# First five pairs' scores in unsplit float32, weight words on GpSimd, early scores in either half of PSUM, and eight spare matmuls of the identity

## The chip, the cores and the metric

The kernel runs on one core of a Trainium2 chip. The metric is device time in microseconds, the median of several runs. A core has five engines with a queue each, worked through in order: PE (TensorE, matrix products into PSUM), DVE (VectorE), ACT (ScalarE), POOL (GpSimd, which doesn't reach PSUM) and SP, which here issues the DMAs. Waits are on semaphores, so an instruction that waits holds up all that stand behind it on its engine.

## The reference

For 8 batches, attention over 8 heads of 576 positions and 64 dimensions, with a threshold close under the row maximum; its output, 576 x 512 per batch, is then mixed over tokens and channels with sines and cosines.

```python
scores = scale * np.matmul(q, k.transpose(0, 1, 3, 2))
thresh = np.max(scores, axis=-1, keepdims=True) - tau
scores = np.where(scores >= thresh, scores, -1000000000.0)
attn = np.exp(scores - np.max(scores, axis=-1, keepdims=True))
attn = attn / (np.sum(attn, axis=-1, keepdims=True) + 1e-09)
x = heads_side_by_side(np.matmul(attn, v))
theta = x @ w_theta
y = w_tok_r @ (x * np.cos(theta)) + w_tok_i @ (x * np.sin(theta))
u = x + y
return u + np.maximum(u @ w_ch, 0.0)
```

The last three steps are taken for each batch. The three weights `w_theta`, `w_tok_r`/`w_tok_i` (both in `w_tok`) and `w_ch` come as float64, 8 bytes a number; all else is float32.

## The kernel before

Two heads make a pair, so there are 32 pairs, 4 to a batch, numbered n = 0 to 31. All numbers are float32, but PE multiplies most of them as "float32r", a rounded form that goes through in one pass. Where accuracy is needed a number x is split into a rounded part and the rest, x = x1 + x2, and the product is taken as x1 y1 + x1 y2 + x2 y1: three one-pass products in place of one plain float32 product.

- `prepare_q` and `prepare_k` load a pair's q and k into `rawq` and `rawk`, round them (a cast on DVE, L705 and L722, or on ACT, L707 and L724) and take the rest (a subtraction, L530, on DVE or POOL). From pair 3 on, DVE first multiplies q by a scalar (`gate`, L696); for pairs 0 to 2 that scalar is applied with the scores.
- `unit(n, i)` takes 128 query rows of both heads (i = 0 to 3) or the last 64 of both (i = 4). PE writes the scores (L759): 12 matmuls of 64 rows x 288 columns, the two heads' each in one half of the array's rows, into four PSUM banks, always banks 0 to 3. DVE copies each head's scores out of PSUM and takes the row extremum along (L780), adds the threshold (L790); ACT makes two passes over them (L804, L811); DVE transposes the result in blocks of 32 (L823, L825) into `a`. "A head" below is one such 128 x 576 block; a pair has 9.
- `values(n)` multiplies `a` by v (L840, 72 plain float32 matmuls on 32-row tiles a call), also into banks 0 to 3. `divide(n)` spreads the inverse row sums over DRAM and multiplies them in (L894, L900).
- `convert` makes two float32r parts of a float64 weight chunk, 13 chunks early on: 4 of `w_theta`, 9 of `w_tok` (4 of `w_ch` follow later). ACT takes the magnitude of the high words (L578), POOL clamps it (L583), DVE builds the float32 bits (L597, L604), the scale of the low word (L611) and the low word times that scale (`word`, L615). ACT rounds the bits (L626); PE adds up bits + word - rounded (L634 to L636), and ACT copies the rest out (L640).
- `mixture(b)` follows once the 4 pairs of a batch are done: channel products (`product`, L948), sines on ACT, transposes (L1091) and the token products (L1136), again with split operands. The first L948 is the first work on PE that needs weights.

Nothing is scheduled at run time: every instruction group is an `Op` in a list, and `ORDER` gives the sequence in which they are emitted, as steps forth and back in that list. `PLACES` gives, for each kind of buffer (`bank` is the PSUM banks), which one each use takes. So the order on every engine is a table of numbers.

## Time and profile before

| | |
|---|---|
| median of 3 runs | 926.42 us (924.15 to 927.21) |
| profiled execution, its own time | 924.78 us |
| its span, first to last instruction | 923.0 us |
| PE, DVE, ACT, POOL busy | 866.0, 714.4, 699.5, 314.3 us |
| mean granted TensorE clock | 0.989 of full speed |

Busy time of PE is modelled for pipelined matmuls, so that it is not PE at its peak. Idle time of an engine that isn't the bottleneck costs nothing. A wait is put down to the releaser that came last.

### The profile page before, as it was taken

The numbers are of one execution on the slowest core, as the hardware profiler recorded it, in microseconds if no ns is written. First come the engines' busy times: TensorE is split into PE (matmuls) and PEld (weight loads), VectorE is DVE, ScalarE is ACT, GpSimd is POOL, SyncE is SP. The second block draws the span as 40 slices with busy tenths as digits, with TensorE's granted clock in tenths as the row PEclk, the third lists the DMA queues.
The fourth block names the chain that finished last, engine by engine and source line by source line (L and its number), as shares of the span: only waits on it lengthen the run. The fifth ranks groups of instructions, "written<-read, shape, count | busy, mean of one in ns | idle before, by whom it ended". The sixth has DMA issues, their size and how long they took to land.

```text
span 923.0 us, 34024 instructions
## 1 busy us (share of the span) xinstructions
PE 866.0 (94%) x14632; PEld 779.5 (84%) x14632; DVE 714.4 (77%) x1598; ACT 699.5 (76%) x1406; POOL 314.3 (34%) x390
## 2 busy tenths in 40 slices
PE   4778799999999999999999999998999999999998
PEld 3556688788898988988999989897989989989898
DVE  7998889987787887778877887777975886876443
ACT  5788898865897678965899659976797659975540
POOL 0212451613443244513244343342334442321202
PEclk9988999999999999999999999999999999999999
DMA  7356535355342364024534351434534243423502
GB/s 261 115 161 224 166 138 178 101 167 178 131 158 93 131 209 175 17 80 151 201 103 144 110 187 67 170 107 143 183 129 129 82 146 122 138 83 131 164 22 75
DMA packets 62375, 126.15 MB, mean 137 GB/s; under 512 B 22512, under 2 KB 31632, under 8 KB 58128
## 3 DMA queue, kind: packets, MB, share of 16 engines
q1 hardware_dynamic: 62080, 123.97, 40.2%
q8 instruction: 115, 1.88, 0.8%
q14 instruction: 36, 0.29, 0.1%
q10 hardware_dynamic: 144, 0.00, 0.0%
HBM read 110.17 MB, written 13.78 MB: 134 GB/s over the span
## 4 chain that ended last, share of the span: by engine, by line
PE 64%; DVE 20%; ACT 8%; issue 3%; DMA 3%; POOL 1%; SPq 0%; DVEq 0%; POOLq 0%; ACTq 0%
PE banks_ps__66 L1136 21%; PE banks_ps__66 L840 14%; PE banks_ps__66 L948 13%; PE banks_ps__66 L759 11%; DVE sc L780 7%; DVE a L823 5%; PE banks_ps__66 L1091 3%; ACT sc L804 2%; ACT s L811 2%; DVE nm L790 1%; PE banks_ps__66 L634 1%; DMA z<-in_w_theta_dram 1%; DVE xl L530 1%; DVE z L1016 1%; DVE zl L1116 1%
## 5 line engine op out<-in xcount | busy, mean ns | idle before, releaser
L804 ACT ACTIVATE sc<-sc,nm 128x576 f32<-128x576 f32 x288 | 216.7, 771 | 78.6 <-DVE nm L790 75.1
L811 ACT ACTIVATE s<-sc,small 128x576 f32<-128x576 f32 x288 | 222.9, 775 | 5.1 <-DVE a L823 0.6
L823 DVE STREAM_TRANSPOSE a<-s 128x576 f32<-128x576 f32 x256 | 189.7, 759 | 35.3 <-PE banks_ps__66 L840 28.6
L759 PE MATMUL banks_ps__66<-k,q 64*128 64x288 f32 (+1 forms) x1728 | 178.7, 320 | 32.7 <-DVE sc L780 24.0
L780 DVE TENSOR_SCALAR_CACHE_REDUCE sc<-banks_ps__66 128x576 f32<-128x576 f32 x261 | 186.2, 741 | 13.2 <-PE banks_ps__66 L759 11.5
L759 PEld LDWEIGHTS banks_ps__66<-k,q 64*128 64x128 f32 (+1 forms) x1728 | 141.4, 194 | 61.1 <-DVE sc L780 37.9
L948 PE MATMUL banks_ps__66<-xh,wm 128*128 128x288 f32 x1024 | 168.9, 302 | 4.2 <-issue 1.6
L840 PE MATMUL banks_ps__66<-a,v 32*64 32x144 f32 x9216 | 165.0, 288 | 4.9 <-DVE sc L780 3.9
L1136 PE MATMUL banks_ps__66<-wt_h,zh 128*128 128x288 f32 x576 | 164.4, 309 | 1.7 <-DVE xT L1148 1.2
L840 PEld LDWEIGHTS banks_ps__66<-a,v 32*64 32x64 f32 x9216 | 146.9, 132 | 18.0 <-issue 9.2
L1136 PE MATMUL banks_ps__66<-wt_l,zh 128*128 128x288 f32 x576 | 160.6, 302 | 0.0
L948 PEld LDWEIGHTS banks_ps__66<-xh,wm 128*128 128x128 f32 x1024 | 143.4, 188 | 14.6 <-issue 8.6
L1066 POOL TENSOR_TENSOR z<-z,xT 128x288 f32<-128x288 f32 x112 | 91.7, 850 | 118.9 <-ACT z L1047 96.4
L1136 PEld LDWEIGHTS banks_ps__66<-wt_h,zh 128*128 128x128 f32 x576 | 108.9, 190 | 6.9 <-issue 3.9
L1136 PEld LDWEIGHTS banks_ps__66<-wt_l,zh 128*128 128x128 f32 x576 | 108.6, 189 | 2.8 <-issue 2.6
L530 POOL TENSOR_TENSOR k<-rawk,k 128x288 fp32r<-128x288 f32 x62 | 52.9, 860 | 168.5 <-DVE k L722 93.0
L530 POOL TENSOR_TENSOR xl<-xT,xh 128x288 fp32r<-128x288 f32 x78 | 66.8, 878 | 109.6 <-ACT xh L907 67.6
L1136 PE MATMUL banks_ps__66<-wt_h,zl 128*128 128x288 f32 x576 | 95.8, 301 | 0.0
L948 PE MATMUL banks_ps__66<-xl,wm 128*128 128x288 f32 x512 | 92.6, 300 | 2.9 <-issue 2.7
L1116 DVE TENSOR_TENSOR zl<-banks_ps__66,zh 128x512 fp32r<-128x512 f32 (+1 forms) x96 | 51.9, 547 | 56.1 <-ACT zh L1097 56.0
L1136 PEld LDWEIGHTS banks_ps__66<-wt_h,zl 128*128 128x128 f32 x576 | 81.5, 188 | 2.9 <-issue 2.4
L948 PEld LDWEIGHTS banks_ps__66<-xl,wm 128*128 128x128 f32 x512 | 75.0, 188 | 7.1 <-issue 6.0
(78 smaller groups left out, 996.3 us busy)
## 6 DMA issues: line engine op xcount, KB each, us to landing
v<-in_vp_dram SPq DMA_DIRECT2D x32, 1152.0 KB
wm<-wm_dram SPq DMA_DIRECT2D x64, 512.0 KB
rawq<-in_qT_dram SPq DMA_DIRECT2D x31, 320.0 KB
rawk<-in_kT_dram SPq DMA_DIRECT2D x31, 288.0 KB
out_dram<-xT SPq DMA_DIRECT2D x31, 288.0 KB
rb<-sums_dram SPq DMA_DIRECT2D x64, 128.0 KB
z<-in_w_tok_dram SPq DMA_DIRECT2D x9, 576.0 KB
wm_dram<-rb SPq DMA_DIRECT2D x16, 256.0 KB
```

The costliest lines, as they stand in the source:

```text
L530: eng.tensor_tensor(out=out()[:, c0:c1], in0=in0()[:, c0:c1], in1=in1()[:, c0:c1], op=ALU.subtract)
L759: nc.tensor.matmul(ps()[:, 2 * j + h, :HS], q[a]()[r, i * P : (i + 1) * P], k[c]()[r, h * HS : (h + 1) * HS], start=(x == 0), stop=(x == 2),)
L780: lambda j=j, sc=sc, scaled=scaled: nc.vector.tensor_scalar(out=sc().rearrange("p (a b) -> p a b", a=2), in0=ps()[:, 2 * j : 2 * j + 2, :H ...
L804: lambda j=j, sc=sc: nc.scalar.activation(out=sc(), in_=sc(), func=AF.Prelu, bias=nm()[:, 2 + j : 3 + j], scale=-1.0, alpha=STEEP),
L811: lambda j=j, sc=sc, total=total, weights=weights: nc.scalar.activation(out=weights(), in_=keys(sc()), func=AF.Exp, bias=back, accum_out=p ...
L823: nc.vector.transpose(out=a()[:, :, j, 32 * i : 32 * i + 32], in_=src.rearrange("p (c q) -> p c q", q=32))
L840: nc.tensor.matmul(ps()[64 * h : 64 * h + 64, b, :w], v()[r, c, h, :], a()[r, c, h, :], start=(c == 0), stop=(c == 17))
L948: nc.tensor.matmul(ps[h]()[:, :HS], wm()[:, a, c, :], parts[c][bb]()[:, h * HS : (h + 1) * HS], start=first and n == 0, stop=final and n = ...
L1066: eng.tensor_tensor(out=zi, in0=zi, in1=x[m]()[:, c0:c1], op=ALU.mult)
L1091: nc.tensor.transpose(out=tp()[:, i * P : (i + 1) * P], in_=z()[:, c : c + P], identity=ident)
L1116: lambda zh=zh, zl=zl, tv=tv: nc.vector.tensor_tensor(out=zl(), in0=tv(), in1=zh().bitcast(F32), op=ALU.subtract),
L1136: nc.tensor.matmul(ps()[:, :HS], zz[c][lo]()[:, zz[c][2]], w[:, c, hs], start=(q + n == 0), stop=(q + n == len(work) - 1),)
```

## The change

For pairs 0 to 4 (`WHOLE = 5`) q and k aren't split: they are loaded straight into the buffers from which PE reads, and the scores are plain float32 products, 4 matmuls to a full unit in place of 12. Pairs 1 to 4 get `gate` multiplied in on POOL, so that only pair 0 applies it with the scores. For the same pairs (`TWICE = 5`) scores and values may stand in banks 0 to 3 or 4 to 7. In `convert`, the first 10 of the 13 early chunks have the low word's product on POOL, as a cast and a product for each half of the chunk, and the first 8 also the rounding of the bits; the factor 2^-52 goes into the matrix that PE multiplies by. `awake` is a matmul of the identity by itself, 256 columns, whose result nobody reads; there are eight of them. `PLACES` and `ORDER` are new all the way through.

```diff
     "wm": (
-        "0101201220220101200012012001201201201201022100121010210210012012011200"
+        "0101201010110202100121021000211021201210210221010210210210201212011201"
...
-    one = const.tile([P, P], F32R, name="one")
-    nc.scalar.copy(out=one, in_=ident)
+    unit_low = const.tile([P, P], F32R, name="unit_low")
+    nc.scalar.mul(out=unit_low, in_=ident, mul=2.0**-52)
...
-        if turn < AT["wp"]:
-            for i in range(2):
-                gps(c_pool(n // 2), lambda i=i: word(nc.gpsimd, n * i // 2, n * (i + 1) // 2), key, (raw, mag), ((w, i),))
-        else:
-            dve(c_two(n), lambda: word(nc.vector), key, (raw, mag), (w,), lock=True)
+        if turn < WORD_POOL:
+            for i in range(2):
+                r = slice(n * i // 2, n * (i + 1) // 2)
+                gps(
+                    c_pool(n // 2) * 0.6, lambda r=r: nc.gpsimd.tensor_copy(out=w()[:, r], in_=lb()[:, r]), key, (raw,),
+                    ((w, i),),
+                )
+                gps(
+                    c_pool(n // 2),
+                    lambda r=r: nc.gpsimd.tensor_tensor(
+                        out=w()[:, r], in0=w()[:, r].bitcast(F32), in1=mb()[:, r].bitcast(F32), op=ALU.mult
+                    ),
+                    key, ((w, i), mag), ((w, i),),
+                )
...
-        act(c_act(n), lambda: nc.scalar.copy(out=hi(), in_=bb().bitcast(F32)), key, (bits,), (hi_b,), hold)
+        if turn < HI_POOL:
+            gps(c_pool(n) * 0.5, lambda: nc.gpsimd.tensor_copy(out=hi(), in_=bb().bitcast(F32)), key, (bits,), (hi_b,), hold=hold)
+        else:
+            act(c_act(n), lambda: nc.scalar.copy(out=hi(), in_=bb().bitcast(F32)), key, (bits,), (hi_b,), hold)
...
-                nc.tensor.matmul(t, one, w()[:, r], start=False, stop=False)
+                nc.tensor.matmul(t, unit_low, w()[:, r], start=False, stop=False)
...
+        if n < WHOLE:
+            q = sb("q", [P, QS])
+            pr.q = (q, q)
...
+            if n:
+                gps(
+                    c_pool(QS) * 0.5, lambda: nc.gpsimd.tensor_scalar(out=q(), in0=q(), scalar1=gate, scalar2=None, op0=ALU.mult), key,
+                    ((q, 0), small_b), ((q, 0),),
+                )
+            return
...
+            places=((0, 4) if n < TWICE else (0,)) if i < 4 else (0, 2), wide=2 * len(heads),
...
-        terms = ((0, 0), (0, 1), (1, 0))
+        whole = n < WHOLE
+        terms = ((0, 0),) if whole else ((0, 0), (0, 1), (1, 0))
...
+    def awake():
+        ps = bank()
+        pe(
+            0.45,
+            lambda: nc.tensor.matmul(
+                ps()[:, :256].rearrange("p (a b) -> p a b", a=2), ident, ident.unsqueeze(1).broadcast_to([P, 2, P]), start=True, stop=True
+            ),
+            0.0, (), (ps,), 4,
+        )
...
+    for _ in range(8):
+        awake()
```

Lines below L450 are numbered higher in the changed kernel: L759 is L801 there, L840 is L882, L780 is L822, L790 is L832, L823 is L865, L583 is L587, L597, L604 and L611 are L601, L608 and L615; L622, L627 and L641 are the new casts, products and roundings on POOL, L714 the product of q and `gate`, L1292 `awake`.

The first place is PE from the program's start. In the kernel before it opens with the scores of the first pair and of 2 units of the second:

```order
L759 MATMUL banks_ps__66<-k,q 128x288 x78
L840 MATMUL banks_ps__66<-a,v 64x144 x72
L871 MATMUL banks_ps__66<-ident,rows 9x128
L634 MATMUL banks_ps__66<-xh,ident 128x512
L635 MATMUL banks_ps__66<-xh,one 128x512
```

In the changed kernel PE begins so:

```order
L1292 MATMUL banks_ps__66<-ident 128x256 x3
L801 MATMUL banks_ps__66<-k,q 128x288 x18
L651 MATMUL banks_ps__66<-xh,ident 128x512
L652 MATMUL banks_ps__66<-xh,unit_low 128x512
L653 MATMUL banks_ps__66<-rb,minus 128x512
L801 MATMUL banks_ps__66<-k,q 128x288 x8
L1292 MATMUL banks_ps__66<-ident 128x256
L882 MATMUL banks_ps__66<-a,v 64x144 x72
```

Three matmuls of the identity now stand first, a pair's scores are 18 matmuls in place of 54, and the first weight chunk is summed up after the first pair's scores, ahead of the first values. Up to the first L948, PE has 252 matmuls L759 before (4 pairs and 3 units) and 90 now (5 pairs); 576 of L840 and 22 weight sums stand ahead of it in both.

The second place is DVE, where the scores begin. Before:

```order
L722 CAST k<-rawk 128x288
L530 TENSOR_TENSOR k<-rawk,k 128x288
L722 CAST k<-rawk 128x288
L705 CAST q<-rawq 128x128
L530 TENSOR_TENSOR q<-rawq,q 128x128
L530 TENSOR_TENSOR k<-rawk,k 128x288
L705 CAST q<-rawq 128x512
L530 TENSOR_TENSOR q<-rawq,q 128x512
L780 TENSOR_SCALAR sc,nm<-banks_ps__66,small 128x576 x2
L705 CAST q<-rawq 128x640
```

Now:

```order
L822 TENSOR_SCALAR sc,nm<-banks_ps__66,small 128x576 x2
L832 TENSOR_SCALAR nm<-nm,small 128x2
L822 TENSOR_SCALAR sc,nm<-banks_ps__66,small 128x576 x2
L832 TENSOR_SCALAR nm<-nm,small 128x2
L601 TENSOR_SCALAR xh<-xl 128x512
L608 SCALAR_TENSOR_TENSOR xh<-wm,xh 128x512
L865 STREAM_TRANSPOSE a<-s_119 128x18x32
L822 TENSOR_SCALAR sc,nm<-banks_ps__66,small 128x576
L615 TENSOR_SCALAR xl<-xh 128x512
```

The splits ahead of and between the scores are gone, and the first weight chunk is worked on after two units; before, that was after six and a half.

The third place is POOL, behind the making of the identity. Before:

```order
L530 TENSOR_TENSOR k<-rawk,k 128x288 x2
L583 TENSOR_SCALAR xl<-xl 128x256 x6
L583 TENSOR_SCALAR xl<-xl 128x288
L530 TENSOR_TENSOR k<-rawk,k 128x288 x2
L583 TENSOR_SCALAR xl<-xl 128x288
```

Now:

```order
L622 CAST xh<-wm 128x256
L587 TENSOR_SCALAR xl<-xl 128x256 x2
L641 CAST rb<-xh 128x512
L622 CAST xh<-wm 128x256
L627 TENSOR_TENSOR xh<-xh,xl 128x256 x2
L714 TENSOR_SCALAR q<-q,small 128x640
L587 TENSOR_SCALAR xl<-xl 128x256
```

The subtractions of k's rest have given way to casts, products and roundings of the weight words and the scaling of q. Over the whole program POOL gets 20 casts, 20 products, 8 roundings and 4 scalings, and loses 8 subtractions of k and 2 of q.

## Rows read from the trace of the kernel before

**Rows 1.** Windows: stretch, length; busy us (count) of each engine; PEclk, DMA share, GB/s.
```profile
0.00:114.70 114.70, 82.26 (x1497) 63.78 (x1497) 99.62 (x230) 89.25 (x184) 28.41 (x52) 0.93 0.57 184
114.70:200.00 85.30, 80.77 (x1332) 71.12 (x1335) 74.92 (x158) 75.31 (x151) 35.35 (x39) 1.00 0.46 149
...
sum 923.00, PE 866.00 PEld 779.48 DVE 714.42 ACT 699.53 POOL 314.28; mean PE 144.33 PEld 129.91 DVE 119.07 ACT 116.59 POOL 52.38
```
**Rows 2.** Waits in 0 to 114.7 us: who for whom: us, times, longest.
```profile
PE banks_ps__66 L759 <- DVE sc L780: 20.1, 16, 2.5
ACT sc L804 <- DVE nm L790: 13.9, 10, 7.0
...
DVE sc L780 <- PE banks_ps__66 L759: 6.6, 11, 1.2
```
**Rows 3.** Groups of DVE, 0 to 114.7 us: busy us, mean ns; idle before, releasers.
```profile
L823 DVE STREAM_TRANSPOSE a<-s 128x576 f32<-128x576 f32 x33 | 24.5, 762 | 2.2 <-ACT s L811 1.3 <-PE banks_ps__66 L840 0.9
L780 DVE TENSOR_SCALAR_CACHE_REDUCE sc<-banks_ps__66,small 128x576 f32<-128x576 f32 x27 | 21.0, 810 | 4.7 <-PE banks_ps__66 L759 4.5
L780 DVE TENSOR_SCALAR_CACHE_REDUCE sc<-banks_ps__66 128x576 f32<-128x576 f32 x13 | 9.3, 748 | 2.3 <-PE banks_ps__66 L759 2.0 <-ACT wt_l L640 0.2
L615 DVE SCALAR_TENSOR_TENSOR xh<-z,xl 128x576 fp32r<-128x576 uint32 (+1 forms) x11 | 8.0, 743 | 0.1
...
L597 DVE TENSOR_SCALAR xh<-xl 128x576 uint32<-128x576 uint32 (+1 forms) x13 | 6.5, 516 | 0.2 <-PE banks_ps__66 L636 0.2
...
L530 DVE TENSOR_TENSOR q<-rawq,q 128x640 fp32r<-128x640 f32 (+2 forms) x5 | 3.4, 687 | 0.1
...
L722 DVE CAST k<-rawk 128x576 fp32r<-128x576 f32 (+1 forms) x5 | 2.0, 398 | 0.6 <-DMA rawk<-in_kT_dram 0.6
L696 DVE TENSOR_SCALAR rawq<-rawq,small 128x640 f32<-128x640 f32 x3 | 1.6, 548 | 0.0
L705 DVE CAST q<-rawq 128x640 fp32r<-128x640 f32 (+2 forms) x4 | 1.6, 405 | 0.0
...
L530 DVE TENSOR_TENSOR k<-rawk,k 128x288 fp32r<-128x288 f32 x2 | 0.9, 455 | 0.0
```
**Rows 4.** Timeline of DVE at the start: start us, us, instruction.
```profile
4.56 0.30 DVE L722 CAST k<-rawk 128x288 fp32r<-128x288 f32 x1
...
7.61 0.82 DVE L780 TENSOR_SCALAR_CACHE_REDUCE sc<-banks_ps__66,small 128x576 f32<-128x576 f32 x1
...
8.36 0.81 DVE L780 TENSOR_SCALAR_CACHE_REDUCE sc<-banks_ps__66,small 128x576 f32<-128x576 f32 x1
```
**Rows 5.** Timeline of PE: two groups of scores.
```profile
5.76 1.81 PE L759 MATMUL banks_ps__66<-k,q 64*128 64x288 f32 x12 [5.76 <-DVE q L705]
...
38.99 1.07 PE L759 MATMUL banks_ps__66<-k,q 64*128 64x288 f32 x12 [1.07 <-ACT xT L856]
```
**Rows 6.** The chain that ended last, two pieces: start us, us, what.
```profile
84.40 0.48 PE banks_ps__66 L634 x2
...
85.15 2.44 PE banks_ps__66 L840 x144
```
**Rows 7.** Groups of POOL, 0 to 114.7 us, columns as in Rows 3.
```profile
L583 POOL TENSOR_SCALAR xl<-xl 128x288 f32<-128x288 f32 (+1 forms) x26 | 11.6, 463 | 44.2 <-ACT xl L578 30.3 <-DMA rb<-sums_dram 9.9 <-issue 4.0
L530 POOL TENSOR_TENSOR k<-rawk,k 128x288 fp32r<-128x288 f32 x9 | 7.7, 862 | 28.9 <-DVE k L722 12.0 <-ACT k L724 8.5 <-PE banks_ps__66 L840 8.4
```
**Rows 8.** Timeline of DVE and POOL about 54 us.
```profile
53.74 0.79 POOL L530 TENSOR_TENSOR k<-rawk,k 128x288 fp32r<-128x288 f32 x1
...
53.76 1.08 DVE L597 TENSOR_SCALAR xh<-xl 128x576 uint32<-128x576 uint32 x1
```
**Rows 9.** Groups of ACT, 0 to 114.7 us, columns as in Rows 3.
```profile
L811 ACT ACTIVATE s<-sc,small 128x576 f32<-128x576 f32 x39 | 30.0, 769 | 0.5
L804 ACT ACTIVATE sc<-sc,nm 128x576 f32<-128x576 f32 x40 | 30.0, 769 | 13.9 <-DVE nm L790 13.9
...
L626 ACT CAST wt_h<-xh 128x576 fp32r<-128x576 f32 x9 | 6.0, 664 | 2.9 <-DVE xh L604 2.9
```

More of the change, by code (lines that the diff above doesn't have):

```diff
@@ L686, in prepare_q @@
         pr = pairs[n]
+        if n < WHOLE:
+            q = sb("q", [P, QS])
+            pr.q = (q, q)
+            for i, (c0, c1) in enumerate(pieces_q(n)):
+                load(
+                    lambda r=slice(c0, c1): nc.sync.dma_start(q()[:, r], qT[n // NP, n % NP][:, r]),
+                    (key if n else -95.0 + 4 * i) + A("raw", n), (), ((q, i),), (c1 - c0) // 2,
+                )
[5 more added lines that the diff above has]
+            return
         raw = sb("rawq", [P, QS])
@@ L714, in prepare_k @@
         pr = pairs[n]
+        if n < WHOLE:
+            k = sb("k", [P, S])
+            pr.k = (k, k)
+            for i, (c0, c1) in enumerate(pieces_k(n)):
+                load(
+                    lambda r=slice(c0, c1): nc.sync.dma_start(k()[:, r], kT[n // NP, n % NP][:, r]),
+                    (key if n else -96.0 + 2 * i) + A("raw", n), (), ((k, i),), (c1 - c0) // 2,
+                )
+            return
         raw = sb("rawk", [P, S])
@@ L760, in score @@
                             ps()[:, 2 * j + h, :HS], q[a]()[r, i * P : (i + 1) * P], k[c]()[r, h * HS : (h + 1) * HS],
-                            start=(x == 0), stop=(x == 2),
+                            start=(x == 0), stop=(x == len(terms) - 1),
                         )
-        pe(
-            6 * c_mm(HS), score, t0 + A("score", n), [
-                *((q[0], c) for c, (c0, _) in enumerate(pieces_q(n)) if c0 <= i * P),
-                *((q[1], [(c, d) for d in range(AT["cut"])]) for c, (c0, _) in enumerate(pieces_q(n)) if c0 <= i * P),
-                k[0], k[1],
-            ],
-            ((ps, list(heads)),),
-            12 * len(heads), mode="r" if i < 4 else "m",
+        pieces = [c for c, (c0, _) in enumerate(pieces_q(n)) if c0 <= i * P]
+        if whole:
+            R = [*((q[0], c) for c in pieces), k[0]]
+        else:
+            R = [*((q[0], c) for c in pieces), *((q[1], [(c, d) for d in range(AT["cut"])]) for c in pieces), k[0], k[1]]
+        pe(
+            0.97 if whole else 6 * c_mm(HS), score, t0 + A("score", n), R, ((ps, list(heads)),),
+            (8 if whole else 12) * len(heads), mode="r" if i < 4 else "m",
         )
```

87 lines of the change are left out of this document (47 added, 40 removed), and 261 rows, old and new, of the table ORDER.

## The prediction

> **What bounds the kernel now.** I read the table of windows first, cut at 114.7 us, where PE starts its first L948 (the chain of waits puts a piece of L948 there). It splits the run in two. From there to the end PE is busy 866.00 - 82.26 = 783.74 of 808.3 us, so it waits for 24.6 us in all: this part is as long as PE's own work. Up to there PE is idle 32.4 us and DVE is busy 99.62 of 114.7 us, ACT 89.25, POOL only 28.41 [rows 1]. The waits of that stretch say who holds whom: PE's scores wait 20.1 us for DVE to have read the banks before, ACT waits 13.9 us for DVE's L790, DVE waits 6.6 us for PE [rows 2]. So the opening is DVE's, and the rest PE's. What DVE is spared in the opening moves the whole rest forward; what happens on DVE, ACT or POOL behind it counts only if PE runs dry. So I work out when the first L948 comes now, and add what PE has still to do then.
>
> **What leaves DVE's opening.** From the groups of DVE [rows 3]:
> - The splits of pairs 0 to 4: subtractions of q 3.4 and of k 0.9 us, all casts of q 1.6 (L705), four of the five casts of k 2.0 - 0.5 = 1.5 (the fifth is pair 5's), and two of three scalings, 2 x 0.548 = 1.1. Sum 8.5 us.
> - The word: 10 of 13 L615 at 0.743 = 7.4 us.
> - L780 with the scalar from memory takes 810 ns, without it 748; 18 of the 27 lose it: 18 x 0.062 = 1.1 us.
>
> Together 17.0 us by the rows. But one instruction's end overlaps the next one's start: two L780 that take 0.82 us stand 0.75 apart [rows 4]. So a tenth goes off: 15.3 us.
>
> At the very start the saving is smaller. Between 4.56 and 7.61 us DVE splits pair 0 [rows 4], and PE starts at 5.76 with 1.81 us of work [rows 5]. Now PE can start when the loads are in (by 4.6 us, since the first cast ran then) and needs some 2.2 us, so DVE's first L780 comes at 6.8, not 7.61: 0.8 us are won where 3.1 x 0.9 = 2.8 of the splits were counted. That takes 2.0 back: 13.3 us.
>
> **The second half of PSUM.** With the next scores already written, DVE should not wait for PE between units: the 6.6 us in 11 waits [rows 2] go, but for one, the first; 6.0 us. Between 0 (if the wait is for something else by then) and 6.6.
>
> **What comes in on DVE before the same point.** The order has 90 score matmuls at 18 a pair ahead of the first L948, 5 pairs and 45 heads; before it was 4 pairs and 3 units with 2 heads each, 42, of which DVE had done 40 (27 + 13) [rows 3]. Five heads more cost 5 x (0.748 + 0.762) x 0.9 = 6.8 us of DVE. They aren't lost: 252 matmuls of 1728 stood ahead, now 90 of 1548, so PE has 18 fewer to do behind, at 12 in 1.07 us [rows 5] 1.6 us.
>
> **What PE pays.** A float32 matmul of 288 columns is two records, 0.48 us at full clock [rows 6]. If the two heads run side by side, as the one-pass ones do, a unit is 2 x 0.48 = 0.96 us plus the same overhead; 12 one-pass matmuls took 1.07 late and 1.81 at the start [rows 5], with the same operands and shapes, so the rate there was lower, whatever the granted clock's mean of 0.93 over the stretch says [rows 1] (full is 2.4 GHz, the lower level 1.2). So 1.2 against 1.07, 2.2 against 1.81: 25 units x 0.15 to 0.4 = 4 to 10 us, and eight identity matmuls of under 0.5 each (256 columns against 288) some 4. PE has 32.4 us idle there to put them in: nothing on the path. Side by side is likely: the values' 144 records of 144 columns, also float32 on part of the rows, take 2.44 us, 17 ns each [rows 6], which is far less than one after the other could.
>
> **What POOL pays, and gives back to DVE.** Neither the casts nor the products are in the trace. The nearest rows: a one-input L583 463 ns, a two-input L530 862 ns [rows 7]. 20 casts at 0.463, 20 products at 0.862, 8 roundings of twice the width at 0.9 and 4 scalings at 1.0 are 37.7 us; 10 subtractions at 0.862 go: +29, POOL at 57 of some 105 us. The bounds for a cast are 0.4 and 0.86 (+8 us): it still fits. But DVE and POOL hinder each other: an L597 that starts 20 ns after a POOL L530 takes 1.08 us, its group's mean being 0.516, so one such meeting costs DVE 0.57 [rows 3, 8]. With POOL's load doubled I take five more of them than before: 3 us. The bounds are none, and all 39 of L597, L611 and L604: 22 us.
>
> The Trainium skill (SBUF — State Buffer, section Who interferes with whom) says that the two engines share a port pair as an exclusive lock, held for a whole instruction, so that a DVE instruction in a two-port mode or with two SBUF inputs blocks and is blocked. By that rule these 39 and nothing from PSUM are exposed; the row about 54 us agrees with it, and 3 us is the sum's value by the rows alone.
>
> ACT: 8 of 13 roundings go, 8 x 0.664 = 5.3, and five heads come, 5 x 2 x 0.769 = 7.7, both times 0.9: 89.25 - 4.8 + 6.9 = 91.4 us [rows 1, 9]. It starts after the first L790, now near 9 us, so it can't be through before 100.4. ACT's first instruction is now the magnitude of a weight chunk, ahead of the first pair's exponentials; that chunk's load stands fifth on SP, behind only pair 0's q and k, so I count no wait, with 2.5 us as the upper bound (DVE then stalls at its first L597).
>
> **Sum.** -13.3 - 6.0 + 6.8 + 3.0 = -9.5: first L948 at 105.2, above ACT's 100.4. With -1.6 behind it, -11.1. The later part has an order of its own, but the same instructions; I leave its 24.6 us of waits as they are. The profiled execution took 924.78 us, its span 923.0; so 913.7 for one like it. The median of the runs stands 1.6 above the profiled one (926.42): 915.3, and I say 915.5.
>
> **Rivals.**
> - ACT or POOL becomes the opening's bound. ACT's 100.4 leaves 4.8 us for waits, and in before it waited 6.9 us for L790 besides the first 7.0 [rows 2]; POOL's words take 2 x 0.862 where DVE's took 0.743, in a queue with the scaling of q. If ACT keeps 6.9 and 3 more for POOL's results, the first L948 is at 110.3: -4.4 - 1.6 = -6.0, 920. Against it: DVE, which made ACT wait, is lighter.
> - More comes of it: no meetings, and DVE's lighter load also takes 3 of the 4.5 us of PE's waits between 114.7 and 200 [rows 1]: -9.5 - 3.0 - 1.6 - 3 = -17, 909; ACT's floor sets the end at 100.4 - 114.7 - 1.6 - 3 = -19, 907.
> - Slower: DVE and POOL in each other's way, at L597, L611 and L604 of the 13 chunks. Each full meeting is 0.57 us; without the 3 us counted the gain is 14.1, so from 25 of 39 on nothing is left, and all 39 give 22 - 14 = +8: 934. Against it: L597's mean of 0.516 says that few of 13 met one [rows 3], at a third of POOL's load to come.
> - The float32 scores don't run side by side. Then a unit is 1.92 us at full clock, 25 units 48 us instead of some 30: PE gets near 100 us of work ahead of L948 and the gain is some 3 us, 922; with much of it at the lower rate, 3.84 a unit, PE needs 25 us more than it has: 945.
> - The order after the opening waits more: if 24.6 us grow by a third, 8 us are given back, 923.5, which reads as no change.
>
> **Chances.** Forecast 0.50, its own range 909 to 921; ACT or POOL bound 0.20; more 0.13; port meetings 0.06; no side by side 0.04; later waits 0.07. The range from 905 to 924 leaves out the two slower cases, the lower end of the third, and little else. About 0.3% (2.8 us) is what a measurement of this kernel can tell from no change. Faster by more: the first three nearly whole and a part of the last two, 0.83; within: most of the last and the edge of the second, 0.09; slower: the meetings and half of no side by side, 0.08.
>
> **What would show it.** The first L948 (now L990) near 105 us. DVE's busy share before it above 0.92, with L780 (L822) no longer waiting for PE. A score unit in float32 near 1.2 us late and 2.2 early: twice that means that the heads follow one another. L597 (L601) with a mean above 0.7 us would mean the port rival; ACT idle less than 5 us after its start, the ACT one. PE idle behind the first L948 near 24 us; above 32 us there, the last rival holds. I'm wrong if the first L948 comes after 112 us, or if it comes at 105 and the end doesn't follow.

## The result and the profile after

The changed kernel takes 914.75 us (median of 4 runs, 913.64 to 915.14) against 926.82 us (924.15 to 927.38) for the one before beside it. The ratio is 0.9873, interval [0.9852, 0.9895]. The forecast was 915.5 us. By the medians the gain is 12.1 us; the two profiled executions, from which all that follows is read, differ by 923.0 - 913.2 = 9.8, as the one before was 2.0 us quicker than its median. Lines of the changed kernel: scores L801 (before L759), their copies L822 (L780), threshold L832 (L790), values L882 (L840), transposes L865 (L823), bits L601, L608, L615 (L597, L604, L611), product of the mixture L990 (L948); on POOL the word's cast and product are L622 and L627, the rounding L641, the scaling of q L714.

The stretches ahead of and behind the first L990, after (it starts at 104.9 us, the last one at 909.0):

```profile
0.00:104.90 104.90, 83.43 (x1441) 59.19 (x1441) 94.88 (x214) 85.20 (x177) 60.21 (x95) 0.95 0.61 203
104.90:909.00 804.10, 781.82 (x13115) 714.27 (x13114) 617.35 (x1357) 606.52 (x1218) 281.23 (x338) 1.00 0.39 130
```

And the second stretch of the kernel before, first product to last:

```profile
114.60:918.80 804.20, 782.99 (x13133) 715.15 (x13132) 614.33 (x1368) 610.39 (x1223) 285.97 (x340) 1.00 0.39 130
```

The whole gain of the profiled executions lies ahead of the first product: 114.6 - 104.9 = 9.7 us. Behind it both kernels take the same 804 us, PE being busy for 782 and 783 of them. POOL's busy time in the opening has doubled, from 28.41 to 60.21 us [rows 1].

Waits in the first 104 us, after, that answer to [rows 2]:

```profile
PE banks_ps__66 L801 <- DVE sc L822: 8.4, 5, 3.0
...
ACT sc L846 <- DVE nm L832: 6.0, 5, 2.1
ACT xl L582 <- DMA wm<-in_w_theta_dram: 6.0, 1, 6.0
...
PE banks_ps__66 L882 <- DVE a L867: 4.3, 2, 4.1
DVE sc L822 <- PE banks_ps__66 L801: 4.0, 4, 2.1
...
PE banks_ps__66 L651 <- DVE sc L822: 3.9, 3, 1.8
```

The wait of PE's scores for DVE went from 20.1 to 8.4 us, but the values now wait 4.3 us for DVE's transposes and the weight sums 3.9 us for DVE to read scores out of the banks. In all PE is idle 104.9 - 83.4 = 21.5 us there, 32.4 before. ACT's wait for L832 went from 13.9 to 6.0, DVE's for PE from 6.6 in 11 waits to 4.0 in 4, of which 2.06 is the very first:

```profile
4.39 0.15 DVE L552 TENSOR_SCALAR small<-small 128x1 f32<-128x1 f32 x1
6.60 0.82 DVE L822 TENSOR_SCALAR_CACHE_REDUCE sc<-banks_ps__66,small 128x576 f32<-128x576 f32 x1 [2.06 <-PE banks_ps__66 L801]
```

PE's float32 units, the first two together and a late one (start, duration; 8 records to a unit):

```profile
4.43 3.10 PE L801 MATMUL banks_ps__66<-k,q 64*128 64x288 f32 x16 [0.17 <-DMA q<-in_qT_dram]
...
65.86 1.24 PE L801 MATMUL banks_ps__66<-k,q 64*128 64x288 f32 x8
```

1.24 us for what would take 8 x 0.24 = 1.92 us in a row (two records of 288 columns are 0.48 us [rows 6]): the two heads run side by side. The first two units take 1.55 us each.

In the kernel before, PE is slow for much longer. The same call of the values takes 4.48 us and, a little later, 2.51:

```profile
29.47 4.48 PE L840 MATMUL banks_ps__66<-a,v 32*64 32x144 f32 x144 [1.66 <-DVE sc L780]
...
35.41 2.51 PE L840 MATMUL banks_ps__66<-a,v 32*64 32x144 f32 x144
```

Its units of scores take 1.81 us or more up to 28 us, against 1.07 from 39 us on [rows 5]. The clock column, which is 1.00 for that stretch, doesn't show this: the trace holds no reading of the clock before 33.7 us there, before 6.3 us in the changed kernel, so that its means for the opening leave these stretches out. What this earlier full rate is worth by itself, no run separates.

Groups of DVE in the first 104 us, after, answering to [rows 3]:

```profile
L822 DVE TENSOR_SCALAR_CACHE_REDUCE sc<-banks_ps__66 128x576 f32<-128x576 f32 x35 | 25.2, 738 | 2.2 <-PE banks_ps__66 L801 1.9 <-ACT s L853 0.3
L865 DVE STREAM_TRANSPOSE a<-s 128x576 f32<-128x576 f32 x32 | 23.2, 754 | 0.7 <-ACT s L853 0.5
L608 DVE SCALAR_TENSOR_TENSOR xh<-z,xh 128x576 uint32<-128x576 uint32 x9 | 7.6, 839 | 0.1
...
L832 DVE TENSOR_SCALAR nm<-nm,small 128x2 f32<-128x2 f32 x19 | 6.6, 346 | 0.3
L615 DVE TENSOR_SCALAR xl<-xh 128x576 uint32<-128x576 uint32 x9 | 5.4, 599 | 0.1
L601 DVE TENSOR_SCALAR xh<-xl 128x576 uint32<-128x576 uint32 x9 | 4.7, 532 | 0.0
...
L608 DVE SCALAR_TENSOR_TENSOR xh<-z,xh 128x512 uint32<-128x512 uint32 x2 | 2.3, 1128 | 0.1
...
L727 DVE TENSOR_SCALAR rawq<-rawq,small 128x640 f32<-128x640 f32 x2 | 1.5, 790 | 0.0
```

The same operations before, kept apart by shape, which [rows 3] doesn't do:

```profile
L604 DVE SCALAR_TENSOR_TENSOR xh<-z,xh 128x576 uint32<-128x576 uint32 x9 | 6.7, 749 | 0.0
L790 DVE TENSOR_SCALAR nm<-nm,small 128x2 f32<-128x2 f32 x18 | 5.1, 285 | 0.1
L597 DVE TENSOR_SCALAR xh<-xl 128x576 uint32<-128x576 uint32 x9 | 4.7, 530 | 0.2 <-PE banks_ps__66 L636 0.2
L611 DVE TENSOR_SCALAR xl<-xh 128x576 uint32<-128x576 uint32 x9 | 4.0, 454 | 0.1
...
L604 DVE SCALAR_TENSOR_TENSOR xh<-z,xh 128x512 uint32<-128x512 uint32 x2 | 1.4, 684 | 0.0
```

The copies out of PSUM (738 against 748 ns) and the transposes (754 against 762) are as before. Most of what works in SBUF beside the busier POOL is longer: 839 against 749, 599 against 454, 346 against 285, 1128 against 684; L601 isn't (532 against 530).

POOL's new work in the first 104 us:

```profile
L627 POOL TENSOR_TENSOR xh<-xh,xl 128x288 fp32r<-128x288 f32 x12 | 10.2, 858 | 7.6 <-DVE xl L615 7.0 <-DVE nm L832 0.5
...
L714 POOL TENSOR_SCALAR q<-q,small 128x640 f32<-128x640 f32 x4 | 7.9, 1986 | 0.0
L622 POOL CAST xh<-z 128x288 fp32r<-128x288 uint32 x12 | 6.0, 497 | 2.3 <-PE banks_ps__66 L652 2.1 <-PE banks_ps__66 L651 0.2
```

### The profile page after: what moved, and what is told of

The parts are those of the page before. It is cut to its first block, busy times and chain, and to the rows that moved or that the text cites. A ratio compares the mean times of both kernels' runs of the same rounds, so it can differ in the third digit from the quotient of the medians.

```text
span 913.2 us, 33850 instructions
## 1 busy us (share of the span) xinstructions
PE 866.1 (95%) x14558; PEld 774.1 (85%) x14558; DVE 713.0 (78%) x1571; ACT 691.7 (76%) x1394; POOL 341.4 (37%) x432
## 4 chain that ended last, share of the span: by engine, by line
PE 57%; DVE 22%; ACT 11%; issue 5%; DMA 2%; POOL 1%; SPq 1%; DVEq 0%; ACTq 0%; POOLq 0%
PE banks_ps__66 L1178 19%; PE banks_ps__66 L990 13%; PE banks_ps__66 L882 12%; PE banks_ps__66 L801 9%; DVE sc L822 7%; DVE a L865 4%; PE banks_ps__66 L1133 3%; ACT s L853 3%; ACT sc L846 3%; DVE nm L832 1%; ACT ang L1024 1%; ACT ang L1010 1%; PE banks_ps__66 L651 1%; DVE xh L608 1%; DVE a L867 1%
## 5 line engine op out<-in xcount | busy, mean ns | idle before, releaser
L822 DVE TENSOR_SCALAR_CACHE_REDUCE sc<-banks_ps__66 128x576 f32<-128x576 f32 x279 | 199.7, 743 | 14.4 <-PE banks_ps__66 L801 13.4
L865 DVE STREAM_TRANSPOSE a<-s 128x576 f32<-128x576 f32 x256 | 187.4, 758 | 27.9 <-PE banks_ps__66 L882 19.5
L801 PE MATMUL banks_ps__66<-k,q 64*128 64x288 f32 (+1 forms) x1638 | 175.7, 323 | 11.3 <-DVE sc L822 9.8
L882 PE MATMUL banks_ps__66<-a,v 32*64 32x144 f32 x9216 | 168.0, 287 | 13.9 <-issue 8.8
L990 PE MATMUL banks_ps__66<-xh,wm 128*128 128x288 f32 x1024 | 171.2, 304 | 3.9 <-DVE xh L951 1.5
L882 PEld LDWEIGHTS banks_ps__66<-a,v 32*64 32x64 f32 x9216 | 147.4, 131 | 29.6 <-issue 19.7
L801 PEld LDWEIGHTS banks_ps__66<-k,q 64*128 64x128 f32 (+1 forms) x1638 | 133.3, 186 | 38.9 <-DVE sc L822 19.3
L1178 PE MATMUL banks_ps__66<-wt_h,zh 128*128 128x288 f32 x576 | 161.1, 304 | 1.1 <-ACT zh L1139 0.8
L990 PEld LDWEIGHTS banks_ps__66<-xh,wm 128*128 128x128 f32 x1024 | 144.5, 189 | 15.8 <-issue 9.4
L1108 POOL TENSOR_TENSOR z<-z,xT 128x288 f32<-128x288 f32 x112 | 89.7, 836 | 99.4 <-ACT z L1089 99.4
L534 POOL TENSOR_TENSOR k<-rawk,k 128x288 fp32r<-128x288 f32 x54 | 47.7, 894 | 141.5 <-ACT k L764 68.9
L990 PE MATMUL banks_ps__66<-xl,wm 128*128 128x288 f32 x512 | 94.5, 302 | 2.1 <-DVE xl L534 1.2
L534 POOL TENSOR_TENSOR q<-rawq,q 128x320 fp32r<-128x320 f32 x54 | 48.3, 907 | 95.8 <-ACT q L738 43.8
```

The costliest lines, as they stand in the source:

```text
L534: eng.tensor_tensor(out=out()[:, c0:c1], in0=in0()[:, c0:c1], in1=in1()[:, c0:c1], op=ALU.subtract)
L801: nc.tensor.matmul(ps()[:, 2 * j + h, :HS], q[a]()[r, i * P : (i + 1) * P], k[c]()[r, h * HS : (h + 1) * HS], start=(x == 0), stop=(x == l ...
L822: lambda j=j, sc=sc, scaled=scaled: nc.vector.tensor_scalar(out=sc().rearrange("p (a b) -> p a b", a=2), in0=ps()[:, 2 * j : 2 * j + 2, :H ...
L865: nc.vector.transpose(out=a()[:, :, j, 32 * i : 32 * i + 32], in_=src.rearrange("p (c q) -> p c q", q=32))
L882: nc.tensor.matmul(ps()[64 * h : 64 * h + 64, b, :w], v()[r, c, h, :], a()[r, c, h, :], start=(c == 0), stop=(c == 17))
L990: nc.tensor.matmul(ps[h]()[:, :HS], wm()[:, a, c, :], parts[c][bb]()[:, h * HS : (h + 1) * HS], start=first and n == 0, stop=final and n = ...
```

## The experiments

The theory at the start: DVE sets the opening, so the gain is what DVE is spared there, part by part, and behind the first product only PE counts. Each run has its own rivals. After the first four runs one more stood beside them: no part gives the gain by itself, but only together with the second PSUM half and an order laid for it. The runs fall into three groups, each on one chip together with the kernel before, whose median was 929.10 us in the first (splits_early to one_half), 927.46 in the second (b_whole, b_words, b_both, late_mix) and 929.73 in the third. Each run's ratio rests on 6 or 12 executions (that of the changed kernel on 4), the moments of the first and the last product on one.

| run | ratio to before, interval | first product | last |
|---|---|---|---|
| changed kernel | 0.9873 [0.9852, 0.9895] | 104.9 | 909.0 |
| splits_early | 1.0006 [0.9983, 1.0028] | 117.0 | 922.3 |
| splits_late | 0.9992 [0.9972, 1.0012] | 105.9 | 923.3 |
| words_dve | 1.0012 [0.9993, 1.0032] | 119.3 | 921.2 |
| one_half | 1.0239 [1.0209, 1.0268] | 137.3 | 943.2 |
| b_whole | 1.0034 [1.0010, 1.0057] | 118.7 | 922.7 |
| b_words | 1.0077 [1.0049, 1.0105] | 122.2 | 930.1 |
| b_both | 1.0058 [1.0034, 1.0083] | 121.8 | 926.0 |
| late_mix | 0.9936 [0.9910, 0.9962] | 106.8 | 917.7 |
| b_two | 1.0275 [1.0242, 1.0308] | 133.7 | 950.2 |
| no_product | 0.9850 [0.9818, 0.9882] | 103.0 | 910.0 |
| no_awake | 0.9833 [0.9803, 0.9863] | 103.8 | 908.0 |
| scores_twice | 0.9863 [0.9825, 0.9901] | 109.4 | 908.9 |

How far such a moment scatters can be read from kernels that share a part. splits_late and late_mix have the changed kernel's opening, and their first product comes at 105.9 and 106.8 us instead of 104.9: up to 2 us tell nothing. Behind the first product splits_early, words_dve, one_half, no_product, no_awake and scores_twice have the changed kernel's instructions, and take 799.5 to 807.0 us (804.1).

### Is DVE the bound of the opening, and only there?

Two runs put DVE work back whose result nobody uses: once in the first pairs, once in pairs 12 to 15.

```diff
+            def spend(j=j, sc=sc):
+                m = n - 0 + 1      # splits_late: n - 12 + 1
+                if j or not 1 <= m <= 4:
+                    return
+                a, b = q[0]()[:, :S].bitcast(F32), k[0]().bitcast(F32)
+                for _ in range(2):
+                    if i == 0 and m >= 3:
+                        nc.vector.tensor_scalar(out=sc(), in0=a, scalar1=gate, scalar2=None, op0=ALU.mult)
...
-                lambda ...: nc.vector.tensor_scalar(
+                lambda ...: spend() or nc.vector.tensor_scalar(
```

> The changed kernel with idle work on DVE: twice the casts, subtractions and scalings of 576 columns that the splits of pairs 1 to 4 had there (8 casts of 0.45, 6 subtractions of 0.75, 4 scalings of 0.49 us: 10.1 us, 9.1 with the overlap taken off), one kind at a time ahead of a unit's first L780 in pairs 0 to 3; the results are overwritten. If DVE sets the end of the opening: the first channel product 7 to 9 us later than 104.9, the time 914.75 + 8 = 922 to 924. If ACT or POOL set it, DVE has some 10 us of idle time to take this in: 915 to 918.

Measured: DVE's busy time ahead of the first product rises by 105.46 - 94.88 = 10.6 us, and the first product comes 12.1 us later. So DVE's work does set the opening, at a little more than one for one. ACT waits for L832 (here L848) for 15.9 us instead of 6.0. The granted clock of the stretch is 0.88 instead of 0.95, and PE's 1441 records take 89.37 us instead of 83.43; whether the surplus comes from that isn't separated. Behind the first product 805.3 us, as before.

> The changed kernel with the same 10.1 us of idle work on DVE, but in pairs 12 to 15, in the middle of the run. If PE alone sets the time there (25.6 us of waits in 808): no change, 914 to 916. If DVE is as tight there as in the opening: 922 to 924, as with the work put early.

Measured: the first product stays at 105.9 us, but 817.4 us lie behind it instead of 804.1, well above the 807.0 that the unchanged part reaches at most. That is 13.3 us for 10 us of DVE work: my claim that behind the first product only PE counts is wrong. Most of it is lost between 300 and 440 us, where PE is busy 127.36 us of 140, against 135.24 in the changed kernel. In one window of that stretch the changed kernel has DVE full:

```profile
320.00:340.00 20.00, 19.53 (x280) 17.39 (x278) 19.75 (x42) 16.35 (x36) 7.08 (x9) 1.00 0.52 186
```

In splits_late PE waits for DVE between 300 and 440 us, where scores had cost the changed kernel 0.3 us of such waits:

```profile
PE banks_ps__66 L801 <- DVE sc L838: 6.2, 10, 1.9
...
PE banks_ps__66 L898 <- DVE sc L838: 1.8, 2, 0.9
```

late_mix puts work on DVE in another place behind the opening: 16 subtractions ahead of those of the token mixture, where DVE waits for ACT.

```diff
-                    lambda ...: nc.vector.tensor_tensor(out=zl(), in0=tv(), in1=zh()...)
+                    lambda ...: (
+                        nc.vector.tensor_tensor(
+                            out=zl()..., in0=x[m]()[:, :512], in1=x[m]()[:, 64:], op=ALU.subtract
+                        ) if nb == 4 and b in (2, 3) else None,
+                        nc.vector.tensor_tensor(out=zl(), in0=tv(), in1=zh()...),
+                    ),
```

> The changed kernel with 16 idle subtractions on DVE of 512 columns (0.68 us each, 10.9 in all), each ahead of one of the mixtures' subtractions L1158 of batches 2 and 3, where DVE waits for ACT anyway (56 us in all behind the opening in the kernel before); results are overwritten. The 10.1 us put ahead of the scores' copies of pairs 12 to 15 cost 11 us. If that was because DVE is full wherever scores are read, and has its idle time in the mixtures: 0 to 3 us, 915 to 918 on the scale of 914.75 (0.987 to 0.990). If any work on DVE counts: 11 us (0.999).

Measured: 810.9 us behind the first product, 6.8 more for 628.00 - 617.35 = 10.7 us of DVE work. Neither expectation holds: even where DVE has idle time beside its own work, some 0.6 of what it is given comes out (a rough figure: 810.9 is 3.9 us above the longest of the six runs with this part unchanged). PE's share of 0.97 behind the opening doesn't mean that other engines are free there.

### What each part is worth

In the changed kernel, the words of the first ten chunks go back to DVE, at the place of POOL's first product:

```diff
-                    ... lambda r=r: nc.gpsimd.tensor_copy(out=w()[:, r], in_=lb()[:, r]), ...
+                    ... lambda r=r: None, ...
-                    lambda r=r: nc.gpsimd.tensor_tensor(... op=ALU.mult),
+                    lambda i=i: i or nc.vector.scalar_tensor_tensor(... op0=ALU.mult, op1=ALU.mult),
```

> The changed kernel with the low words' product of the first 10 chunks back on DVE, one instruction a chunk at the place in the order of the first product on POOL; POOL's 20 casts and 20 products are gone. By the forecast's terms DVE gets 7.4 x 0.9 = 6.7 us back, less what the meetings with POOL cost it: DVE's L601, L608, L615, L832 and others took 6.4 us more than their like in the kernel before, of which the 24 us of words on POOL should make most, some 4. So 2.5 us slower, 917. If POOL's words cost DVE as much as they spare it: 914 to 915. If POOL sets the opening's end: faster, 911.

Measured: 14.4 us later for 7.9 us of DVE work; the whole gain is gone. DVE isn't fuller, but emptier (85.31 of the first 104 us instead of 94.01): waits of each engine for the others have grown, and PE now waits for DVE's words, ACT for a weight load:

```profile
PE banks_ps__66 L652 <- DVE xh L627: 8.9, 4, 5.5
ACT xl L582 <- DMA z<-in_w_tok_dram: 8.7, 2, 6.9
DVE sc L822 <- PE banks_ps__66 L801: 7.2, 4, 3.7
```

Next, the changed kernel with scores and values of pairs 0 to 4 all in banks 0 to 3, each engine's order kept but for instructions that had to move because a bank wasn't free:

```diff
-                    b.slot = int(next(places[b.cls.name]))
+                    b.slot = int(next(places[b.cls.name])) * (not b.low)
...
+        ps.low = n < TWICE and i < 4    # scores; values: n < TWICE
```

> The changed kernel with the scores and values of pairs 0 to 4 in banks 0 to 3 alone, as before the change; where two of them stood in the two halves at once, the later one is moved behind the readers of the earlier one (a handful of places on PE and DVE). If the second half is worth the 6.0 us that I counted: 919 to 921, with DVE's waits for PE's scores back near 6 us from 4.0. If DVE is full anyway and finds other work in that time: 915 to 916.

Measured: the first product 32.4 us later, ratio 1.0239. DVE, 0.90 busy in the changed kernel, is busy 64.00 of the first 104 us, and the granted clock is 0.79 in them instead of 0.95; PE and DVE take turns:

```profile
DVE sc L865 <- PE banks_ps__66 L844: 26.1, 15, 6.3
PEld banks_ps__66 L844 <- DVE sc L865: 23.4, 15, 4.3
```

I had priced the second half by DVE's waits before, 6.6 us. That is what it costs in an order that was made for one half. In this order it costs five times that.

The other way round, from the kernel before: unsplit float32 scores alone (b_whole), the words on POOL alone (b_words), and both (b_both), again with the order of before.

```diff
+        if n < 5:            # b_whole: q and k loaded straight into the operand buffers
+            q = sb("q", [P, QS])
+            pr.q = (q, q)
+            ...
-        terms = ((0, 0), (0, 1), (1, 0))
+        terms = ((0, 0),) if n < 5 else ((0, 0), (0, 1), (1, 0))
-            dve(c_two(n), lambda: word(nc.vector), key, (raw, mag), (w,), lock=True)
+            if turn < 10:    # b_words: cast and product on POOL
+                gps(c_two(n), word_pool, key, (raw, mag), (w,))
+            else:
+                dve(c_two(n), lambda: word(nc.vector), key, (raw, mag), (w,), lock=True)
```

> The kernel before with one part of the change alone: q and k of pairs 0 to 4 unsplit, loaded straight into the buffers that PE reads, scores in float32; gate is applied with L780 for these five pairs (18 heads more than before at 62 ns). Everything else, the words, the single half and the order on every engine, is that of before, with the splits taken out of it. If DVE sets the opening's end even in the old order: 8.5 x 0.9 = 7.7 us less, 2.0 of it not gained at the start, 1.1 back for gate: 4.5 us faster than before (ratio 0.995). If the gain needs the new order: no change (0.999 to 1.001). If float32 costs PE: slower.

Measured: the first product at 118.7 us, 4.1 later than before, though DVE has 7.3 us less work ahead of it (92.25; 99.52 before). The spared time became a wait:

```profile
DVE sc L844 <- PE banks_ps__66 L823: 13.7, 12, 2.2
```

against 6.6 [rows 2]. My theory fails here. The ratio, 1.0034, lies above the 0.999 to 1.001 of a gain that only needs the new order, and has the sign of the last rival, float32's cost on PE. That rival is borne out: for the same 4 pairs and 3 units PE's scores take 41.4 us ahead of the first product instead of 34.1. The added wait lies in the first 35 us, this run and then the kernel before:

```profile
DVE sc L844 <- PE banks_ps__66 L823: 9.7, 7, 2.2
```

```profile
DVE sc L780 <- PE banks_ps__66 L759: 3.2, 6, 0.7
```

There a float32 unit takes 2.29 us where the split one took 1.81 [rows 5]; late it takes 1.24. The first two units and a late one, then the second unit of the kernel before:

```profile
4.44 2.29 PE L823 MATMUL banks_ps__66<-k,q 64*128 64x288 f32 x8 [4.44 <-DMA q<-in_qT_dram]
8.39 2.29 PE L823 MATMUL banks_ps__66<-k,q 64*128 64x288 f32 x8 [1.66 <-DVE sc L844]
...
49.01 1.24 PE L823 MATMUL banks_ps__66<-k,q 64*128 64x288 f32 x8 [0.92 <-DVE sc L844]
```

```profile
9.23 1.81 PE L759 MATMUL banks_ps__66<-k,q 64*128 64x288 f32 x12 [1.66 <-DVE sc L780]
```

From the first start to the second it is 3.95 us, and 3.47 before: the 0.48 us by which the unit has grown. PE and DVE take turns on the one half, so a longer unit comes out as time, and the lead of 1.3 us at the first unit is a lag of 1.6 at the seventh (26.83; 25.27 before). In the changed kernel most units take 1.24 us from 17 us on.

> The kernel before with the words of the first 10 chunks on POOL alone (20 casts, 20 products), in the old order. DVE is spared 7.4 x 0.9 = 6.7 us and loses some 4 to meetings with POOL: 2.7 us faster (0.997). If POOL's longer way (four instructions where DVE had one) delays PE's sums, which wait for the words: slower by up to 3 us (1.003).

Measured: 1.0077, slower, with the sign of the rival but more than its 1.003. DVE's busy time ahead of the first product falls by only 2.2 us (97.31; 99.52 before), though 7.4 us of words are gone. POOL works its queue in order, so the clamp for the next chunk stands behind words that wait, and DVE behind the clamp:

```profile
DVE sc L791 <- PE banks_ps__66 L770: 10.8, 15, 2.3
POOL xh L627 <- DVE nm L801: 8.0, 4, 3.8
...
DVE xh L597 <- POOL xl L583: 7.2, 3, 2.7
```

> The kernel before with both of these parts. If the shares add up: 7 us faster than before (0.992). What is then missing to the changed kernel's 0.987 is the second half of PSUM, the roundings on POOL and the new order, some 4 to 5 us. If single parts are worth nothing in the old order: 0.999.

Measured: 1.0058. DVE has 10.8 us less work ahead of the first product (88.72) and waits 15.0 us for PE, 9.9 of them in the first 35 us as in b_whole, and 5.0 for POOL. The two parts together, worth -7 by my sum, cost 7 us in the first product in the order of before.

What b_whole lacks might have been the second half of PSUM, so b_two adds it for every second unit:

```diff
-                    b.slot = int(next(places[b.cls.name]))
+                    b.slot = int(next(places[b.cls.name])) + 4 * b.high
...
+        ps.high = n < 5 and i in (1, 3)
```

> The kernel before with two parts of the change: the first five pairs' scores in unsplit float32 (as in the run b_whole), and every second score unit of these pairs in PSUM banks 4 to 7 instead of 0 to 3; word weights, values and the order of each engine's work stay as before. Theory (the spared DVE work turned into a wait for the one PSUM half): DVE's waits for scores fall from 13.7 to about 7 us, the first product comes at about 112 us instead of 118.7, the time is about 924 us (ratio 0.995 to 0.999). Rival (the small tiles that the old order sends through banks 4 to 7 now hold the scores up, so a second half is worth nothing without an order made for it): waits for scores 12 us or more, or as many microseconds in new waits of DVE and PE for those small tiles, first product at 117 us or later, ratio 1.002 or more.

Measured: 1.0275, the worst of all; the first product at 133.7 us. Up to 133 us DVE waits 19.1 us for scores and PE waits for DVE in two places, the second being the sums of the weight chunks that take turns with scores in the upper banks:

```profile
PE banks_ps__66 L825 <- DVE sc L846: 15.1, 5, 4.7
PE banks_ps__66 L677 <- DVE sc L846: 9.2, 5, 3.5
```

So the second half is worth nothing, and costs 15 us against b_whole, in an order that puts small tiles into those banks at any time. Another 12 us are lost behind the first product (816.5 us; 804.0 in b_whole); what loses them is open. The rival's direction holds; its size was far above what I allowed. This run doesn't say what the new order with its new places is worth by itself: that can't be had without the parts, since it is made for their durations.

### What hides the added work

> The changed kernel without GpSimd's 20 products of the first ten chunks' words; their casts stay (the word is then the rounded low word alone, so the output is another). Theory (DVE sets the opening, and GpSimd beside it makes DVE's instructions longer): 14 us of GpSimd work go, DVE's 512-column copies of the scores and its 576-column subtractions beside it shrink from 1.13 and 0.84 us towards 0.75, DVE has 2 to 4 us less, the first product comes 2 to 4 us earlier (about 102), ratio against the kernel before 0.983 to 0.985, some 3 us under the changed kernel. Rival one (the meetings come from GpSimd's scalings and roundings, or cost only where DVE has slack): first product within 1 us, ratio 0.987. Rival two (the chain cast, product, word matmul, mean is on the path): 6 us or more earlier.

```diff
-                    lambda r=r: nc.gpsimd.tensor_tensor(out=w()[:, r], ... op=ALU.mult),
+                    lambda: None,
```

Measured: POOL is spared 60.21 - 45.97 = 14.2 us, the first product comes 1.9 us earlier, which is within the scatter, the last one 1.0 later; the time can't be told from the changed kernel's. DVE's groups in the first 104 us:

```profile
L608 DVE SCALAR_TENSOR_TENSOR xh<-z,xh 128x576 uint32<-128x576 uint32 x9 | 7.6, 847 | 0.1
...
L601 DVE TENSOR_SCALAR xh<-xl 128x576 uint32<-128x576 uint32 x9 | 5.2, 584 | 0.4 <-PE banks_ps__66 L650 0.4
L615 DVE TENSOR_SCALAR xl<-xh 128x576 uint32<-128x576 uint32 x9 | 5.1, 568 | 0.1
...
L608 DVE SCALAR_TENSOR_TENSOR xh<-z,xh 128x512 uint32<-128x512 uint32 x2 | 1.5, 754 | 0.1
```

The two longest fell from 1128 to 754 ns, L615 from 599 to 568, but L601 rose from 532 to 584 and the nine L608 stay at 847. So taking the products away doesn't shorten most of them, and wins no time: rival one holds. Which POOL instructions meet them isn't shown: the nine L608 take 752 ns in words_dve, where casts and products are both gone, but 744 (L604 there) in b_words, which has both. (The expectation calls the 512-column L608 a copy of scores; it builds weight bits.)

> The changed kernel without the 20 matmuls of the identity. Theory (they stand where TensorE is idle and DVE sets the time; a lower granted clock stretches only score and word matmuls that DVE mostly doesn't wait for): the granted clock between 20 and 60 us falls from 0.91 to 0.75 to 0.85, the first product comes 0 to 2 us later, ratio against the kernel before 0.987 to 0.990. Rival one (the clock is what the change lives by: at half clock the float32 units of 1.24 us take 2.2 and DVE waits for them): first product 5 us or more later, ratio 0.993 or more. Rival two (they delay the matmuls queued behind them): faster, ratio 0.985 or less.

```diff
-            lambda: nc.tensor.matmul(ps()[:, :256]..., ident, ident..., start=True, stop=True),
+            lambda: None,
```

(The run leaves out all eight identity matmuls there are; the 20 is a slip.) Measured: first product 1.1 us earlier, last one 1.0 earlier, ratio 0.9833. That lies in the range of rival two, but its interval overlaps that of the changed kernel: nothing that can be told apart. Windows at 20 us, changed kernel and this one:

```profile
20.00:40.00 20.00, 16.61 (x339) 11.16 (x339) 18.03 (x41) 16.47 (x37) 12.12 (x17) 0.91 0.46 149
```

```profile
20.00:40.00 20.00, 16.52 (x337) 11.89 (x337) 19.22 (x43) 17.06 (x37) 11.73 (x17) 0.83 0.44 143
```

The same window in late_mix and splits_late, which have the changed kernel's opening:

```profile
20.00:40.00 20.00, 15.99 (x339) 10.63 (x339) 18.23 (x39) 16.43 (x35) 11.74 (x17) 0.91 0.44 136
```

```profile
20.00:40.00 20.00, 17.23 (x339) 11.85 (x339) 17.95 (x39) 16.15 (x35) 11.73 (x17) 0.83 0.43 137
```

So 0.91 and 0.83 both occur with the eight matmuls, and this window's clock says nothing about them. At the very start they do show: without them the first four units take 7.07 us and the trace's first reading of the clock comes at 9.8 us, in the changed kernel, splits_late, late_mix and no_product they take 6.05 to 6.66 us and the reading comes at 6.2 to 7.5. No time was won by it.

> The changed kernel with the score matmuls of two of the four units of each of the first five pairs made twice, into the same banks: 10 units more of about 1.24 us, 12.4 us of TensorE work in the opening, no other engine's work changed. Theory (DVE sets the opening, and TensorE has 18.5 us of idle time in its first 104 us, much of it waits for DVE): a third or less comes out as time, first product 0 to 4 us later, ratio against the kernel before 0.987 to 0.992. Rival (with DVE nearly full and each unit's matmuls right ahead of DVE's copy of them, the path alternates between the two): first product 8 to 12 us later, ratio 0.996 to 1.000.

```diff
-            for x, (a, c) in enumerate(terms):
+            for x, (a, c) in [*enumerate(terms)] * (2 if whole and i in (1, 3) else 1):
```

Measured: 92.03 - 83.43 = 8.6 us more of PE ahead of the first product, which comes 4.5 us later; the last one comes at 908.9, as in the changed kernel (909.0), since only 799.5 us lie between. The time is that of the changed kernel within its interval. So PE has room in the opening for about half of what it was given, less than the theory's two thirds and far more than the rival allowed. That the 4.5 us were made good behind the first product isn't shown, since that part scatters by as much.

No run was faster than the changed kernel by more than the intervals allow. Not tried by themselves: the new order without the parts, the roundings and the scaling of q on POOL, and work put on ACT.

## Why the prediction was right, and where it wasn't

The forecast of 915.5 us came out at 914.75, and its place was right: the first product at 105.2 foretold, 104.9 found. That the number is met to 0.8 us is in part luck, and three terms of the opening were off by 3 to 4 us, with different signs. By its steps:

- **The number.** The profiled executions differ by 9.8 us, nearly all of it in the opening; I had 11.1, with 1.6 us behind it that didn't come. I also added 1.6 us because the median before stood that far above the profiled execution; after the change it stands 0.2 below (914.75; 914.95). The two misses cancel.
- **DVE bounds the opening.** Right: splits_early. Of the signs, DVE's share there is 0.90, not above 0.92, and L822 still waits 4.0 us for PE.
- **The sum of DVE's work.** By the terms the sum was 99.6 - 15.3 + 6.8 + 3.0 = 94.1 us of busy time ahead of the first product; 94.88 was found. But two terms were off in opposite directions. Five heads more (+6.8): there are 44 copies instead of 40, and no more transposes than before, 37; so 4 x 0.738 x 0.9 = 2.7. I took it that what PE has been given ahead of a point DVE has also finished. The meetings with POOL (+3): from the group means above 9 x 0.090 + 9 x 0.145 + 19 x 0.061 + 2 x 0.444 = 4.2, and with the smaller groups about 6. That leaves 2 us. About 0.9 of them are one scaling and one cast of q that I took off and that still stand ahead of the first product (L727 runs twice and L736 once; I had counted one scaling as left and no cast). The rest I can't place; the tenth taken off for overlap is a rough figure.
- **Waits of DVE.** 15.1 - 6.0 + 2.0 = 11.1 us of idle time foretold, 104.9 - 94.9 = 10.0 found. Its wait for PE fell by 2.6 rather than 6.0; the rest of the fall is in what it waited for ACT, for the values and for loads.
- **The second half as a term of 6 us.** Wrong as a price: DVE's wait fell by 2.6. Taking the half away in the new order costs 32 us (one_half), adding it to b_whole in the old one costs 15 (b_two). It is a condition of the order, not a term.
- **A sum of parts.** Here lies the step that held only by the order behind it: the parts tried in the old order make the kernel slower, alone or together (b_whole, b_words, b_both, b_two), and two of them undone in the new one give back all the gain or more (words_dve, one_half); the identity matmuls undone give back nothing (no_awake). What made the sum come out is, I take it, that the new order was laid for the new durations, so that DVE stays 0.90 busy; no run shows the order apart from the parts. I had read from it where the work stands and took it for granted that it would fit.
- **Behind the first product PE alone counts.** Wrong: each microsecond of DVE work there costs 0.6 to 1.3 (late_mix, splits_late). The forecast survived as the change leaves that part as it was, 804 us. Of the 1.6 us that PE was to save there, PE's busy time shows 1.2, and the waits took them: to the end PE is idle 808.3 - 782.7 = 25.6 us, near the 24 foretold.
- **PE's float32 units.** Right late, 1.24 us against 1.2. The first two take 1.55 each against 2.2; 2.2 is right for an order like the one before (2.29 in b_whole), where PE stays slow up to 34 us. The mean clock of 0.93 that I doubted [rows 1] has no reading in it before 33.7 us. scores_twice shows room on PE for half of 8.6 us more.
- **POOL.** +29 us to 57 foretold, 60.2 found. The scaling of q takes 1.99 us where I said 1.0.
- **The theta load: no wait of ACT, 2.5 at most.** The row says 6.0 us. It cost little, as ACT's first work beside it, the first exponentials, had to wait for L832 until 8.4 us.
- **The rivals.** ACT still waits 6.0 us for L832, near the 6.9 of the first rival, but only 1.0 for POOL's results where that had 3; that ACT sets nothing is read from its 85.20 busy of 104.9 us, no run put work on it. The port rival's sign, L601 above 0.7 us, isn't there (0.532). The Trainium skill (SBUF — State Buffer, section Who interferes with whom) has DVE's instructions with two SBUF inputs or in a two-port mode exposed to POOL and the others not. The rows after the change agree in part: copies from PSUM and transposes are as before, L608, with two inputs, is longer (749 to 839 ns), and of the one-input ones L615 is (454 to 599) and L601 isn't (530, 532). Even the two-column L832 goes from 285 to 346; which of the one-input ones run in a two-port mode no row shows.

## What to carry to other kernels

Here, where one engine was 0.87 busy and the others waited for it, its spared work told within some microseconds how much earlier the next stage could start, with the order of all queues laid anew for the new durations; a part tried in the old order can lose although it takes work from the bottleneck. Price a buffer by the run without it in the order that uses it, not by the waits of the kernel that never had it. And a share of 0.97 on one engine doesn't free the others: put work on them in the place in question before calling it hidden. A moment read from one execution needs a second kernel with the same stage beside it, and a clock column a look at the durations of the same matmuls early and late.
